# Merging one PSUM tile, moving one values step, and cutting the last output piece in three

## The chip, the cores and the metric

The kernel runs on one core of a Trainium2 chip. The metric is the device time in microseconds; before the change it is 170.12 us, the median of 3 runs (170.12 to 170.14). The engines named below are TensorE (PE, with its weight loads PEld), VectorE (DVE), ScalarE (ACT), GpSimd (POOL) and SyncE (SP). SP and ACT issue the output transfers, POOL the loads of the inputs.

## The reference, cut to what matters

Block-sorted attention over 4 batches with 8 heads of 768 positions, followed by a maxout layer. All inputs and the output are float32.

```python
P = sort_net                                   # (4, 8, 8, 8)
for _ in range(5):                             # Sinkhorn: rows, then columns
    P = np.exp(P - P.max(-1, keepdims=True))
    P = P / (P.sum(-1, keepdims=True) + 1e-09)
    P = P / (P.sum(-2, keepdims=True) + 1e-09)
k_sorted = np.einsum('bhij,bhjcd->bhicd', P, k_b)   # blocks of 96 positions
v_sorted = np.einsum('bhij,bhjcd->bhicd', P, v_b)
scores = scale * q_b @ k_sorted.T                   # within a block
attn = softmax(scores)
x = (attn @ v_sorted)                               # to (3072 tokens, 512)
h1, h2 = x @ w1, x @ w2                             # 512 -> 1024
out = np.maximum(h1, h2) @ w_out                    # 1024 -> 512
```

## The kernel before, in words

The maxout is computed as relu(x (W1 - W2)) Wout + x (W2 Wout). So the kernel needs, besides the difference of the two weights, the small product W2 Wout, 512 x 512, once. For it W2 is transposed on PE (`w2_transposes`, L525, in two calls of 16 transposes each, into the PSUM tiles `tw_ps` and from there into the SBUF tile `w2T`), and four products (`w_product`, L556, PSUM tile `wc_ps`) of eight matmuls of 512 columns each run over the eight row blocks of `w2T` in order and give the four parts of `wc`. The first call of `w2_transposes` fills row blocks 0 to 3 of `w2T`; the second, the one that the change touches, fills blocks 4 to 7.

All PSUM tiles come from one pool of four buffers, of two banks each, taken in turn (`psum`, L61). A tile can be taken only when what was read out of the tile four places before is through. A copy out of PSUM is `evac` (L98): on ACT at L103 or on DVE at L105.

A batch goes through sorting of K and V (`sort_k`, `sort_v`), scores and their exp (`scores`, eight units of a batch), attention times V (`values`, L463: eight matmuls, and on DVE a reciprocal and a multiplication that gives a part of `x`), the transposes of x (`x_transposes`, L496; of the first batch on PE through PSUM tile `tx_ps`, four calls), the hidden layer (`moe_h`, tiles `h_ps` and `g`) and the output (`moe_out`, tile `out_ps`, 12 matmuls for each 128 tokens: eight over `g` with Wout and four over the transposed x with `wc`). V is brought into another order before its sorting by copies on DVE, the turns (`turn_v`, L203; twelve positions of a block at a time for later batches, L707).

The order of the work is written by hand: each engine's instructions stand in the order in which the Python program issues them, and nothing moves them. In the loop over batches (L748) the units of a batch's maxout are issued one by one; after unit n come the steps of `tail[n]` (L716), and then as many steps of the next batch's attention as are due. In the first batch unit 3 is the last hidden unit of the first half of the tokens, units 4 and 5 are the first two W2 Wout products, and `tail[3]` holds, between them: values of unit 6, the second call of the W2 transposes, values of unit 7, a transpose of x, and three turns. The call has the letters "AD": the first eight transposes go to a PSUM tile of their own that ACT empties, the last eight to another that DVE empties.

The last 256 tokens of the last batch are put out in pieces by `moe_out_last` (L632): for each piece 12 matmuls over its columns into a PSUM tile, a copy on ACT (L640) or DVE (L642), and a DMA of the piece to the output (L643), issued from ACT where ACT copied and from SP otherwise. Before the change tokens 4 x 128 onward go as one piece of 512 columns, and the last 128 tokens as a piece of 384 columns on DVE and one of 128 columns on ACT.

Of the kernel before, what the change touches and what calls it, by code (L numbers as in the profile page):

```python
# [9 lines left out]

FP32 = mybir.dt.float32
BF16 = mybir.dt.bfloat16


@with_exitstack
def kernel(
# [16 lines left out]
    nc = tc.nc  # L33
# [4 lines left out]
    B, H, S, D = q.shape  # L38
# [26 lines left out]
    def ps_f32(name):  # L65
        return psum.tile([128, 1024], FP32, tag="ps", name=name)

    def ps_bf16(name):
        return psum.tile([128, 2048], BF16, tag="ps", name=name)

    fill = const.tile([128, 512], BF16, tag="fill", name="fill")
    nc.vector.memset(fill, 0.0)  # L72
# [11 lines left out]
    def late_zeros(by):  # L84
        late[by] = const.tile([128, 128], BF16, tag=f"late{by}", name="late")
        nc.vector.memset(late[by], 0.0)
# [11 lines left out]
    def evac(out_ap, in_ap, n, two_x=False, eng=None):  # L98
        a_ns, d_ns = (200 + n) / 1.2, (130 + (n / 2 if two_x else n)) / 0.96
        if eng:  # L100
            load[eng] += a_ns if eng == "A" else d_ns
        if (eng or pick(a_ns, d_ns)) == "A":
            nc.scalar.copy(out=out_ap, in_=in_ap)  # L103
        else:
            nc.vector.tensor_copy(out=out_ap, in_=in_ap)  # L105
# [9 lines left out]
    for b in range(2):  # L115
        kT[b] = big.tile([128, 32 * BLK + 32], BF16, tag=f"kT{b}", name="kT")
        kT[b + 2] = kT[b]
        nc.vector.memset(kT[b][:, 32 * BLK :], 0.0)
    v_dc = big.tile([128, D * BLK + 32], BF16, tag="v_dc", name="v_dc")
    nc.vector.memset(v_dc[:, D * BLK :], 0.0)  # L120
    e_bufs = []
    for n in range(NE):
        t = big.tile([BLK, 8 * BLK + 32], BF16, tag=f"e{n}", name=f"e{n}")
        nc.vector.memset(t[:, 8 * BLK :], 0.0)
# [34 lines left out]
    w2_sb = big.tile([128, HP, DFF], BF16, tag="w2", name="w2_sb")  # L159
# [16 lines left out]
    ident = const.tile([128, 128], BF16, tag="ident", name="ident")  # L176
# [26 lines left out]
    def turn_v(rows, eng, c0, c1, d0=0, d1=D):  # L203
        dst = v_dc[rows, 0 : D * BLK].rearrange("p (d c) -> p d c", c=BLK)[:, d0:d1, c0:c1]
        src = v_raw[rows].rearrange("p (c d) -> p d c", d=D)[:, d0:d1, c0:c1]
        if eng == "A":
            nc.scalar.copy(out=dst, in_=src)
        else:
            nc.vector.tensor_copy(out=dst, in_=src)  # L209


    rowsum = const.tile([G, NB], FP32, tag="rowsum", name="rowsum")
# [309 lines left out]
    w2T = big.tile([128, NFB, DMODEL], BF16, tag="w2T", name="w2T")  # L522
    wc = big.tile([128, HP, DMODEL], BF16, tag="wc", name="wc")

    def w2_transposes(t, eng):  # L525

        w = 16 // len(eng)
        outs = []
        for p, e in enumerate(eng):
            ps = ps_bf16("tw_ps")  # L530
            for n in range(w):
                fb, dmt = t * 4 + (p * w + n) // 4, n % 4
                nc.tensor.matmul(  # L533
                    ps[:, n * 128 : (n + 1) * 128],
                    w2_sb[:, dmt, fb * 128 : (fb + 1) * 128],
                    ident,
                    is_transpose=True,
                    start=True,
                    stop=True,
                )  # L540
            outs.append((ps, p, e))

        def out():
            for ps, p, e in outs:
                fb = t * 4 + p * w // 4
                evac(
                    w2T[:, fb : fb + w // 4, :].rearrange("p f d -> p (f d)"),
                    ps[:, 0 : w * 128],
                    w * 128,
                    two_x=True,  # L550
                    eng=e,
                )

        return out
# [77 lines left out]
    def moe_out_last(ti, pieces):  # L632

        tok0 = (B - 1) * S + ti * 128
        for n0, n1, eng in pieces:
            ps = ps_f32("out_ps")
            out_products(ps[:, 0 : n1 - n0], B - 1, ti, n0, n1)
            o = opool.tile([128, n1 - n0], FP32, tag=f"o{ti}{n0}", name="o", bufs=1)
            if eng == "A":
                nc.scalar.copy(out=o, in_=ps[:, 0 : n1 - n0])  # L640
            else:
                nc.vector.tensor_copy(out=o, in_=ps[:, 0 : n1 - n0])  # L642
            (nc.scalar if eng == "A" else nc.sync).dma_start(  # L643
                out=out[tok0 : tok0 + 128, n0:n1], in_=o
            )


    def att(b):

        SC = [lambda u=u: scores(b, u) for u in range(8)]  # L650
        VA = [lambda u=u: values(b, u) for u in range(8)]
        TR = [lambda t=t: x_transposes(b, t) for t in range(4)]
        return SC, VA, TR
# [20 lines left out]
    SC, VA, TR = att(0)  # L674
# [37 lines left out]
    def load_rest():  # L712
# [5 lines left out]
        2: [SC[6], SC[7], VA[5]],  # L718
        3: [
            VA[6],  # L720
            lambda: w2_transposes(1, "AD")(),
            VA[7],
            lambda: x_transposes(0, 2, "A"),
            lambda: [turn(second, c) for c in (0, 12, 24)],
        ],
# [22 lines left out]
    for b in range(B):  # L748
        units = [lambda t=t: moe_h(b, 0, t, None if b else "A") for t in range(4)]
        if b == 0:  # L750
            units[0] = lambda: None
            units[1] = lambda: None
        wps = [lambda dmt=dmt: w_product(dmt, "A" if dmt == 1 else None) for dmt in range(4)]
        if b == 0:
            units += wps[:2]
        units += [lambda t=t: moe_h(b, 1, t) for t in range(4)]
        cost = [1.3] * 8
        if b == 0:
            units += wps[2:]
            cost[4:4] = [1.7] * 2  # L760
            cost += [1.7] * 2
        units += [
            lambda ti=ti, part=part: moe_out(b, ti, part)
            for ti in range(6 if b < B - 1 else 4)
            for part in range(2)
        ]
        cost += [1.3] * 12
        if b == B - 1:
            units += [
                lambda: moe_out_last(4, [(0, 512, "D")]),  # L770
                lambda: moe_out_last(5, [(0, 384, "D"), (384, 512, "A")]),
            ]
        steps, lo = [], 2
        load["A"] = load["D"] = 0.0
        if b < B - 1:
            qs = [lambda half=half: q_transposes(1, half) for half in range(2)]
            if b < 2:
                tail[18 - 4 * b] = [lambda two=two: pair_q(b + 2, two) for two in range(2)]
                tail[18 - 4 * b] += [lambda half=half: q_transposes(b + 2, half) for half in range(2)]
            ks = [lambda t=t, b=b: sort_k(b + 1, t) for t in range(3)]  # L780
            SC, VA, TR = att(b + 1)

            def group(*fs):
                return [lambda: [f() for f in fs]]

            if b == 0:
                lo = 10
                tail[9][2:2] = ks
                vs = [lambda t=t: sort_v(1, t) for t in range(4)]
                tns = [lambda c=c: turn(both, c) for c in range(0, BLK, 12)]  # L790
                for step, n in [((VA, 0), 0), ((VA, 1), 1), ((VA, 2), 2), ((VA, 4), 3), ((TR, 1), 4), ((VA, 5), 5), ((SC, 7), 6), ((VA, 6), 7)]:
                    step[0][step[1]] = lambda f=step[0][step[1]], g=tns[n]: (f(), g())
                steps = group(*vs[:3]) + qs[:1] + group(*SC[0:2], vs[3]) + qs[1:] + VA[:1]
                steps += group(*SC[2:5]) + VA[1:2]
            elif b == 1:
                vs = [lambda t=t: sort_v_pair(2, t) for t in range(8)]
                steps = group(*ks) + group(*vs[:2]) + group(*SC[0:2], late_loads)
                steps += group(*vs[2:4]) + group(*vs[4:6]) + group(*vs[6:]) + group(*SC[2:4]) + VA[:2]
            else:
                steps = group(*ks) + group(*SC[0:2])  # L800
                steps += VA[:1] + group(*SC[2:5]) + VA[1:2]
            rest = SC[4:] if b == 1 else SC[5:]
            steps[-1:] = group(VA[1], TR[0])
            steps += VA[2:3] + group(VA[3], TR[1])
            steps += group(*rest[:-1]) + VA[4:5] + rest[-1:] + group(VA[5], TR[2])
            steps += VA[6:7] + group(VA[7], TR[3])
        done = 0
        for n, unit in enumerate(units):
            unit()
            for step in tail.get(n, []):  # L810
                step()
            total = sum(cost[lo:-2])
            want = -(-len(steps) * sum(cost[lo : n + 1]) // total)
            while done < min(want, len(steps)):
                steps[done]()
                done += 1
        tail = {}
# [28 lines left out]
```

The softmax here doesn't subtract the row's maximum and nothing guards it: scores larger than these inputs give would overflow.

## Time and profile before

| what | value |
|---|---|
| median of 3 runs | 170.12 us |
| profiled execution | 170.12 us, of it 168.3 us span (first to last instruction) |
| DVE, ACT busy | 92.2 us (55%), 80.2 us (48%) |
| chain that ended last, by engine | PE 90%, DVE 6%, DMA 1%, ACT 1%, issue 1% |
| chain, largest lines | out_ps L607 38%, h_ps L580 26%, wc_ps L559 4%, tw_ps L533 1% |
| granted PE clock | 1.00 |
| output DMAs at the end: 512, 384, 128 columns | 256, 192, 64 KB; 2.0, 1.9, 1.7 us from issue to landing |

The chain of waits is followed back from the last instruction, at each step to what released it. A timeline row gives start, length, engine, line, operation, written and read tiles, and in brackets the idle time before and what ended it. PE matmuls are pipelined, and their ends are modelled, so a group's length includes the run-out of its last matmul where another engine waits for it. A row with x8 merges eight instructions.

### The profile page before, as it was taken

What the parts mean: (1) busy time and instruction counts of PE and PEld (TensorE: products, weight loads), DVE (VectorE), ACT (ScalarE), POOL (GpSimd) and SP (SyncE); (2) the same over time, 40 slices, a digit from 0 to 9 for tenths busy, and PEclk for the clock granted to TensorE, in tenths of its full rate; (3) what the DMA queues carried; (4) which work ended last, traced back from release to release, by engine and by line L of the source; (5) the groups of instructions that cost most, each with busy time, mean ns of one, the idle gap of its engine ahead of it and who ended that gap; (6) DMA issues with size and microseconds to landing.
All of it is one profiled execution on the core that took longest, in us unless ns stands there. A gap on an engine that the chain in (4) does not pass through costs nothing.

```text
span 168.3 us, 4525 instructions
## 1 busy us (share of the span) xinstructions
PE 162.1 (96%) x2003; PEld 96.7 (57%) x2003; DVE 92.2 (55%) x198; ACT 80.2 (48%) x99; POOL 25.0 (15%) x40
## 2 busy tenths in 40 slices
PE   7799999999999999999999999999999999999992
PEld 7738766746666554457665545576554545654452
DVE  4979686699256589847674448074452322240041
ACT  3598976855874554046773350446605404311000
POOL 7954372124200000000500000000000000000000
PEclk9999999999999999999999999999999999999999
DMA  3999999999999864990199349930024183000333
GB/s 49 199 204 208 198 207 206 209 193 205 216 217 200 138 177 70 210 265 36 14 198 168 95 124 210 210 114 6 0 51 129 46 214 126 2 0 0 125 125 125
DMA packets 29666, 23.09 MB, mean 137 GB/s; under 512 B 16656, under 2 KB 24592, under 8 KB 29648
## 3 DMA queue, kind: packets, MB, share of 16 engines
q0 software_dynamic: 10304, 12.58, 44.2%
q1 hardware_dynamic: 19200, 10.17, 24.2%
q8 instruction: 15, 0.25, 0.6%
q10 hardware_dynamic: 144, 0.07, 0.1%
q14 instruction: 3, 0.02, 0.0%
HBM read 25.17 MB, written 6.29 MB: 187 GB/s over the span
## 4 chain that ended last, share of the span: by engine, by line
PE 90%; DVE 6%; DMA 1%; ACT 1%; issue 1%
PE out_ps L607 38%; PE h_ps L580 26%; PE o_ps L471 5%; PE wc_ps L559 4%; PE k_ps L377 4%; PE s_ps L444 4%; PE v_ps L398 2%; PE v_ps L419 1%; PE tw_ps L533 1%; DMA p_sb<-in_sort_net_dram 1%; PE tx_ps L509 1%; PE tq_ps L352 1%; PE tq_ps L347 1%; DVE colsum L226 1%; PE o_ps L81 1%
## 5 line engine op out<-in xcount | busy, mean ns | idle before, releaser
L607 PE MATMUL out_ps<-wo_sb,g 128*128 128x512 bf16 (+2 forms) x200 | 48.1, 371 | 0.0
L580 PE MATMUL h_ps<-xT,w_sb 128*128 128x384 bf16 x256 | 44.8, 326 | 0.2 <-ACT g L594 0.2
L580 PEld LDWEIGHTS <-w_sb 128*128 128x128 bf16 x256 | 24.0, 98 | 15.8 <-issue 0.2
L452 ACT ACTIVATE e<-s_ps 96x768 bf16<-96x768 f32 x32 | 24.2, 804 | 16.1 <-PE s_ps L444 15.9
L607 PEld LDWEIGHTS <-g 128*128 128x128 bf16 x200 | 17.0, 97 | 15.7
L594 ACT ACTIVATE g<-h_ps 128x768 bf16<-128x768 f32 x21 | 16.9, 811 | 18.4 <-PE h_ps L580 18.4
L607 PE MATMUL out_ps<-wc,xT 128*128 128x512 bf16 (+2 forms) x100 | 24.8, 370 | 0.0
L103 ACT COPY o<-out_ps 128x1024 f32<-128x1024 f32 x9 | 9.1, 1012 | 30.0 <-PE out_ps L607 25.7
L596 DVE TENSOR_SCALAR g<-h_ps 128x768 bf16<-128x768 f32 x11 | 10.5, 955 | 22.6 <-PE h_ps L580 22.6
L488 DVE TENSOR_TENSOR x<-o_ps,rs 96x512 bf16<-96x512 f32 x32 | 22.0, 686 | 1.1
L482 DVE RECIPROCAL rs<-o_ps 96x8 f32<-96x8 f32 x32 | 6.4, 200 | 19.8 <-PE o_ps L471 19.8
L607 PEld LDWEIGHTS <-xT 128*128 128x128 bf16 x100 | 9.6, 97 | 11.2
L209 DVE COPY v_dc<-v_raw 64x768 bf16<-64x768 bf16 (+2 forms) x18 | 15.6, 898 | 0.4 <-DMA v_raw<-in_v_dram 0.3
L471 PEld LDWEIGHTS <-e 96*128 96x128 bf16 x256 | 11.7, 97 | 6.6 <-ACT e L452 0.5
L471 PE MATMUL o_ps<-v_sb,e 96*128 96x65 bf16 x256 | 13.1, 193 | 0.1
L105 DVE CAST v_sb<-v_ps 96x1024 bf16<-96x1024 f32 x7 | 8.5, 1213 | 4.7 <-PE v_ps L398 4.2
L103 ACT CAST v_sb<-v_ps 96x1024 bf16<-96x1024 f32 x9 | 8.9, 1013 | 1.1 <-PE v_ps L419 1.0
L444 PEld LDWEIGHTS <-kT 64*128 64x128 bf16 x256 | 6.0, 94 | 5.3 <-issue 4.6
L444 PE MATMUL s_ps<-qT,kT 64*128 64x96 bf16 x256 | 8.5, 204 | 0.1
L81 PEld LDWEIGHTS <-fill 128*128 128x128 bf16 x109 | 7.1, 122 | 2.2 <-DVE fill L72 1.2
L105 DVE COPY o<-out_ps 128x1024 f32<-128x1024 f32 x2 | 2.5, 1225 | 10.6 <-PE out_ps L607 9.5
L103 ACT CAST kT<-k_ps 128x1024 bf16<-128x1024 f32 x8 | 7.7, 1021 | 1.1 <-PE k_ps L377 1.1
(76 smaller groups left out, 138.3 us busy)
## 6 DMA issues: line engine op xcount, KB each, us to landing
out_dram<-o SPq DMA_DIRECT2D x11, 512.0 KB, 3.1
k_raw<-in_k_dram POOLq DMA_DIRECT2D x12, 256.0 KB, 10.4
q_raw<-in_q_dram POOLq DMA_DIRECT2D x4, 768.0 KB, 12.5
v_raw<-in_v_dram POOLq DMA_DIRECT2D x6, 384.0 KB, 13.6
w_sb<-in_moe_w_dram POOLq DMA_DIRECT2D x3, 512.0 KB, 15.8
wo_sb<-in_moe_w_out_dram POOLq DMA_DIRECT2D x2, 512.0 KB, 19.5
v_raw<-in_v_dram POOLq DMA_DIRECT2D x3, 256.0 KB, 4.9
w_sb<-in_moe_w_dram POOLq DMA_DIRECT2D x2, 256.0 KB, 14.1
```

Source lines behind the costliest of these rows:

```text
L81: nc.tensor.matmul(ps[:, 0:w], w0, fill[:, 0:w], start=True, stop=True)
L103: nc.scalar.copy(out=out_ap, in_=in_ap)
L105: nc.vector.tensor_copy(out=out_ap, in_=in_ap)
L209: nc.vector.tensor_copy(out=dst, in_=src)
L444: nc.tensor.matmul(ps[:, h2 * 512 + ii * 128 : h2 * 512 + ii * 128 + BLK], kT[b][rows, (hp * 8 + i) * BLK : (hp * 8 + i) * BLK + 128], rhs ...
L452: nc.scalar.activation(out=e[:, 0 : 8 * BLK].rearrange("p (t c r) -> p t c r", t=8, r=R), in_=ps[0:BLK].rearrange("p (t f) -> p t f", t=8) ...
L471: nc.tensor.matmul(ps[:, h2 * 512 + ii * 65 : h2 * 512 + (ii + 1) * 65], e[:, (h2 * 4 + ii) * BLK : (h2 * 4 + ii) * BLK + 128], v_sb[:, m0 ...
L488: nc.vector.tensor_tensor(out=x, in0=ov[:, :, :, 0:D], in1=rs.to_broadcast([BLK, 2, 4, D]), op=ALU.mult,)
L580: nc.tensor.matmul(h_ps[t][:, m * 512 : m * 512 + TCH], w1_sb[:, hp, fb * 128 : (fb + 1) * 128], xT[:, b % 2, ch, hp % 2, hp // 2, :], sta ...
L594: nc.scalar.activation(out=g, in_=src, func=AF.Relu)
L596: nc.vector.tensor_scalar(out=g, in0=src, scalar1=0.0, scalar2=None, op0=ALU.max)
L607: nc.tensor.matmul(dst, g_tiles[b, ch, m // 2][:, m % 2, off : off + 128] if m < NFB else xT[:, b % 2, ch, hp % 2, hp // 2, off : off + 12 ...
```

## The change

Four edits. `turn_v` gets a repeat loop with a count of 1. `w2_transposes` takes one PSUM tile for all sixteen transposes of a call, and copies it out in as many column ranges as the call has letters; for the first call (one letter) that is what it did before, for the second ("AD") two tiles of eight transposes become one tile with two copies. In `tail[3]` the values of unit 7 are issued ahead of that second call, no longer behind it. The last 128 tokens go out in three pieces of 256, 128 and 128 columns, on ACT, DVE and ACT, in place of two of 384 and 128 on DVE and ACT.

```diff
+TWICE = 1
...
-        if eng == "A":
-            nc.scalar.copy(out=dst, in_=src)
-        else:
-            nc.vector.tensor_copy(out=dst, in_=src)
+        for _ in range(TWICE):
+            if eng == "A":
+                nc.scalar.copy(out=dst, in_=src)
+            else:
+                nc.vector.tensor_copy(out=dst, in_=src)
...
     def w2_transposes(t, eng):
-
-        w = 16 // len(eng)
-        outs = []
-        for p, e in enumerate(eng):
-            ps = ps_bf16("tw_ps")
-            for n in range(w):
-                fb, dmt = t * 4 + (p * w + n) // 4, n % 4
-                nc.tensor.matmul(
...
-            outs.append((ps, p, e))
-
+        ps = ps_bf16("tw_ps")
+        for n in range(16):
+            fb, dmt = t * 4 + n // 4, n % 4
+            nc.tensor.matmul(
...
         def out():
-            for ps, p, e in outs:
-                fb = t * 4 + p * w // 4
+            w = 2048 // len(eng)
+            for n, e in enumerate(eng):
                 evac(
-                    w2T[:, fb : fb + w // 4, :].rearrange("p f d -> p (f d)"),
-                    ps[:, 0 : w * 128],
-                    w * 128,
+                    w2T[:, t * 4 : t * 4 + 4, :].rearrange("p f d -> p (f d)")[
+                        :, n * w : (n + 1) * w
+                    ],
+                    ps[:, n * w : (n + 1) * w],
+                    w,
                     two_x=True,
                     eng=e,
                 )
...
             VA[6],
+            VA[7],
             lambda: w2_transposes(1, "AD")(),
-            VA[7],
             lambda: x_transposes(0, 2, "A"),
...
-                lambda: moe_out_last(5, [(0, 384, "D"), (384, 512, "A")]),
+                lambda: moe_out_last(5, [(0, 256, "A"), (256, 384, "D"), (384, 512, "A")]),
```

More of the change, by code (lines that the diff above doesn't have):

```diff
@@ L525, in w2_transposes @@
     def w2_transposes(t, eng):
-        w = 16 // len(eng)
-        outs = []
-        for p, e in enumerate(eng):
-            ps = ps_bf16("tw_ps")
-            for n in range(w):
-                fb, dmt = t * 4 + (p * w + n) // 4, n % 4
[L533 to L540, printed above, removed]
-            outs.append((ps, p, e))
+        ps = ps_bf16("tw_ps")
+        for n in range(16):
+            fb, dmt = t * 4 + n // 4, n % 4
+            nc.tensor.matmul(
+                ps[:, n * 128 : (n + 1) * 128],
+                w2_sb[:, dmt, fb * 128 : (fb + 1) * 128],
+                ident,
+                is_transpose=True,
+                start=True,
+                stop=True,
+            )
         def out():
-            for ps, p, e in outs:
-                fb = t * 4 + p * w // 4
+            w = 2048 // len(eng)
+            for n, e in enumerate(eng):
                 evac(
-                    w2T[:, fb : fb + w // 4, :].rearrange("p f d -> p (f d)"),
-                    ps[:, 0 : w * 128],
-                    w * 128,
+                    w2T[:, t * 4 : t * 4 + 4, :].rearrange("p f d -> p (f d)")[
[3 more added lines that the diff above has]
+                    w,
                     two_x=True,
```

## The prediction

> **What bounds the kernel now.** I read the page's first two parts, then the chain of waits, then the timeline at the two places that the change touches, last the DMA view of the end.
>
> ```profile
> span 168.3 us, 4525 instructions
> PE 162.1 (96%) x2003; PEld 96.7 (57%) x2003; DVE 92.2 (55%) x198; ACT 80.2 (48%) x99; POOL 25.0 (15%) x40
> ```
>
> TensorE (PE) is busy 96% of the span, and the row PEclk of the page is full in every slice. From 38 to 113 us the chain is PE alone; so whatever PE loses or gains at one place is carried to the end, unless a later PE wait absorbs it, and there are only two small ones (0.07 us at 113.89, about 0.2 us at 117.5 behind an activation that itself follows PE). The rest of the span is the start (12.6 us), and what follows the last product. First place, the chain in the stretch of 30 to 40 us (start, length, what):
>
> ```profile
> 32.46 0.90 PE tw_ps L533 x16
> 33.36 0.24 PE o_ps L471 x8
> 33.60 0.39 PE tx_ps L509 x8
> 34.00 0.02 issue
> 34.02 1.89 PE wc_ps L559 x8
> 35.91 0.34 PE tx_ps L509 x8
> 36.25 1.73 PE wc_ps L559 x8
> ```
>
> The reader is to see two unequal twins: the first W2 Wout product with its gap takes 1.91 us and the second 1.73, the tx group before it 0.39 against 0.34. PE loses 0.19 + 0.05 = 0.24 us here. The timeline of 29 to 40 us tells why:
>
> ```profile
> 32.96 1.01 ACT L103 COPY w2T<-tw_ps 128x1024 bf16<-128x1024 bf16 x1
> 33.40 0.69 DVE L105 COPY w2T<-tw_ps 128x1024 bf16<-128x1024 bf16 x1
> 34.23 0.69 DVE L488 TENSOR_TENSOR x<-o_ps,rs 96x512 bf16<-96x512 f32 x1
> 35.25 3.03 DVE L209 COPY v_dc<-v_raw 64x768 bf16<-64x768 bf16 x4 [0.33 <-DMA v_raw<-in_v_dram]
> ```
>
> The two copies overlap. The first wc_ps is the fourth PSUM tile after the one that the ACT copy reads; with four buffers it takes the same one, and starts at 34.02, just after that copy's end (33.97). Second place, the end, in the timeline from 161 us:
>
> ```profile
> 163.76 0.81 PE L607 MATMUL out_ps<-wc,xT 128*128 128x384 bf16 x4
> 164.41 0.61 PE L607 MATMUL out_ps<-wo_sb,g 128*128 128x128 bf16 x8
> 164.61 0.56 DVE L642 COPY o<-out_ps 128x384 f32<-128x384 f32 x1 [1.26 <-PE out_ps L607]
> 165.28 0.27 ACT L640 COPY o<-out_ps 128x128 f32<-128x128 f32 x1 [9.33 <-PE out_ps L607]
> 165.57 0.37 ACTq L643 DMA_DIRECT2D out_dram<-o  x1
> ```
>
> The last 128 columns go PE, ACT, DMA. In the DMA windows of 166.5 to 166.6 (two lines) and 166.8 to 166.9 (one), with packets, MB and share of the 16 DMA engines, q1 is SP's queue with the 384-wide piece, and q10 is ACT's:
>
> ```profile
> q1 hardware_dynamic: 26, 0.03, 84.0%
> q10 hardware_dynamic: 8, 0.00, 13.6%
> ...
> q10 hardware_dynamic: 39, 0.01, 51.0%
> ```
>
> The last small piece starts while the wide one still fills the engines. The last bytes move at 166.92, and the span ends 1.38 us later with no data moving.
>
> **What the Trainium skill says.** "PSUM — Partial Sum Buffer", sections "Specifications (TRN2)" and "PSUM bank collisions raise a hardware error": a bank holds 2 KiB per partition, two engines must not be on the same bank at once, and different banks are free. The halves of the merged tile (1024 bf16 each) are two banks, so the chip would let both copies run together; before, the copies overlap from 33.40 to 33.97 out of two tiles. No trace of before shows two copies out of one tile. "DMA: Bandwidth & Descriptors", section "Anatomy of one DMA — SWDGE (gpsimd) path": a fixed part of about 2 us, mostly the confirmation of the last write. That section is for POOL's path; here the three last output pieces, from SP and ACT, land 1.7 to 2.0 us after issue, with sizes of 64 to 256 KB, so the fixed part rules here too. Its section "Issuing engines are not separate DMA queues" says that they all share 16 engines and interleave: the shares of q1 and q10 above show it.
>
> **The change, part by part.**
>
> 1. The repeat count of 1 in turn_v adds nothing. No W2 Wout product changes its tile, and no turn moves; what changes are the second half of the W2 transposes, the place of one values step, and the last output piece.
>
> 2. The middle. PE has the same instructions, values(7) now ahead of the transposes. In the built program's order both copies now hang on each other: ACT's waits for the sixteenth transpose (before: the eighth), VectorE's (DVE) for ACT's copy (before: for its own eight transposes). One PSUM tile fewer is taken, so the first wc_ps now takes the buffer of values(6), free at 33.43: the bank wait goes. Step by step, on the clock of the trace of before:
> values(6) ends at 32.46. Its successor values(7) needs the exp that ended at 32.11, and runs to 32.70 (0.24). The transposes run to 33.60 (0.90), tx to 33.94 (0.34). The x multiplication of values(7) follows its twin on DVE from 33.43 and is through about 34.35, no cover lost.
> ACT starts at 33.64 (hop 0.04, as from wc_ps at 35.91 to its copy at 35.95) and ends at 34.65 (1.01). DVE follows at 34.68 and ends at 35.37 (0.69).
> The first wc_ps matmul could start at 33.78 (a group's last matmul has its modelled end 0.16 after the next may start). At 0.216 each, the fifth would start at 34.64; it needs ACT's half, at 34.69: +0.05. The seventh would then start at 35.12; it needs DVE's half, at 35.42: +0.30. The eighth starts at 35.64 and ends at 36.02. Before: 35.91. So +0.11 us: 0.24 of old waits go, 0.35 of new ones come.
> What stands behind: ACT's tx copy moves from 34.03 to about 34.66 and ends at 35.46, ahead of the wc copy at about 36.06, and its first reader is at 38.1. The DVE turns start at 35.37 in place of 35.25, their v_raw having landed; four of them end 0.12 later at 38.4, and the block-diagonal work behind them has its reader (sort_k) at 43.4. DVE idles 2.27 us before 44.40, waiting for a load of q, which absorbs it. POOL's load of v_raw at 42.42 waits for a turn and moves by 0.1. No PE wait for such a load is in the chain.
> The unknown is the size of the hand-overs and whether the new waits cost what their copies last. Lower bound -0.24 (all old waits go, none comes: it needs DVE's half by 35.1). Upper bound +0.45: three hops of 0.15 in place of 0.04. I take +0.11.
>
> 3. The end. Twelve 384-wide products become twelve of 256 and twelve of 128. Spacings in the trace: 384 wide, (164.41 - 162.46) / 12 = 162.5 ns; 128 wide, 0.45 / 8 = 56; six of 512 take 1.30, so 216. For 256 the skill's formula ("TensorE: Matmul & The Clock Gate", section "Back-to-back issue gap", N / 2.4 + 2.5) gives 109, and it fits the other three. 12 x (109 + 56 - 162.5) = +0.03 us. The twelve more weight loads hide: 98 ns each in the row of L607, yet the 128-wide products go every 56.
> ACT's 256-wide copy is not in this trace; 266 ns for 128 and 0.59 us for 512 (wc at 35.95) give an estimate of 0.37. It runs 163.97 to 164.34, its DMA issue to 164.73, and ACT then waits for the last copy until 165.31: 0.58 us of cover. The DVE piece of 128, 0.29 by the slope between its 512 and 384 copies (691 and 558 ns), ends at 164.93. The third tile takes a buffer that DVE emptied at 161.36. No wait.
> Bytes follow an issue by 0.85 us (163.38 to 164.23, and 165.20 to 166.05 in the DMA windows). So the 128 KB move from about 165.2 to 165.6, the middle 64 KB from 165.8 to 166.1, and the last 64 KB, issued at 165.60, from 166.45, alone: 0.23 us of each engine (15.3% of 1.5 us in the DMA view of 165.8 to 167.3) and 0.11 of stagger (the 256 KB took 0.80 for 0.69 busy) end at 166.79. Before: 166.92. So the piece that finishes last gains 0.13 net of the 0.03. Bounds: gain 0.24 (no stagger, net) and loss 0.03 (its start was never delayed by the wide piece).
>
> Sum: +0.11 - 0.13 = -0.02 us. The profiled execution took 170.12 us itself (span 168.3 and 1.8 around it), the median of the runs: 170.1 us.
>
> **Rivals.** I call no change what lies within 0.2%, 0.34 us, about what this measurement tells apart.
> A, slower: the new chain transposes, ACT, DVE, PE is longer than the sum of its rows. For it: three hand-overs in series where PE had the two copies side by side, and no row for two copies of one tile. Against it: hops of 0.02 to 0.05 everywhere in the chain. With 0.15 a hop the middle costs 0.45, and with no gain at the end 170.12 + 0.45 + 0.03 = 170.6 us. It decides once DVE's half is ready 0.2 us later than 35.42.
> B, faster: PE finds both halves in time, as it would if ACT did start after eight transposes, and the last piece gains its whole 0.24: 170.12 - 0.24 - 0.24 = 169.64 us. For it: the bank wait really goes. Against it: the wait for the sixteenth transpose.
> C, the end loses its gain alone because the piece's own latency set it: +0.11 + 0.03, 170.26 us, still no change.
>
> **How the numbers follow.** Forecast with C on its edge: 0.66 in all, 169.85 to 170.4. A: 0.23, since a chain in series has more ways to grow than to shrink. B: 0.11. The range reaches to A's 170.55 and, on the other side, to 169.75. Faster 0.11, same 0.66, slower 0.23.
>
> **What would show it.** In the changed trace: DVE's w2T copy starts after ACT's has ended, about 34.7, with ACT named as its releaser; the first wc_ps group lasts about 2.1 us, its start near 33.95; ACT's 256-wide copy near 164.0; q1 and q10 no longer share a window at the end; last bytes about 1.2 us after the last ACT issue and not 1.35. Wrong it would be if PE shows a wait over 0.5 us before the first wc_ps ends, or if the last piece lands 1.7 us after issue as now.

## The result, and the profile after

The changed kernel takes 170.85 us, the median of 6 runs (170.41 to 171.02), against 170.13 us for the kernel before beside it: a ratio of 1.0042, with a 95% interval of 1.0029 to 1.0055. It is slower by 0.72 us. The profiled execution took 171.01 us, of it 169.2 us span, 0.9 us more than the span before.

That 0.9 us has two places. The first is the middle; this is the chain of waits of the changed kernel from 30 to 40 us:

```profile
32.23 0.49 PE o_ps L473 x16
32.71 0.91 PE tw_ps L531 x16
33.62 0.02 issue
33.65 1.02 ACT w2T L104
34.67 0.02 issue
34.69 0.70 DVE w2T L106
35.39 0.05 issue
35.44 0.60 PE wc_ps L557 x2
36.05 0.34 PE tx_ps L511 x8
36.39 1.73 PE wc_ps L557 x8
```

The chain, which ran on PE alone here before, now leaves PE for the two copies of `w2T`, one behind the other, and comes back for the last two of the eight products (x2). The tx group that follows starts at 36.05 in place of 35.91, so PE is 0.14 us late, and it stays so: the second W2 Wout product, and every later group of the chain up to the last pieces, has the same shift. The twelve more products at the end add 0.03.

The other 0.72 us come after PE has stopped. The timeline of the changed kernel, last rows:

```profile
165.45 0.27 ACT L638 COPY o<-out_ps 128x128 f32<-128x128 f32 x1 [0.97 <-PE out_ps L605]
165.75 0.61 ACTq L641 DMA_DIRECT2D out_dram<-o  x1
```

The last copy starts 0.17 us later than before (0.14 + 0.03), and so does its issue, give or take 0.01. From that issue to the end of the span it was 168.3 - 165.57 = 2.73 us before; now it is 169.2 - 165.75 = 3.45. The DMA view from 155 us on (KB each, and us from issue to landing) shows why:

```profile
out_dram<-o SPq DMA_DIRECT2D x1, 256.0 KB, 4.0
out_dram<-o ACTq DMA_DIRECT2D x1, 128.0 KB, 3.4
out_dram<-o SPq DMA_DIRECT2D x1, 64.0 KB, 3.0
out_dram<-o ACTq DMA_DIRECT2D x1, 64.0 KB, 2.5
```

All four last pieces land late, the 256 KB one too, which the change doesn't touch (2.0 us before). And queue q8, which the profile calls the instruction queue, moves one packet here that was not there before: a piece of the program itself. The page of the kernel before and that of the changed one have these lines for q8, over the whole run:

```profile
q8 instruction: 15, 0.25, 0.6%
```

```profile
q8 instruction: 16, 0.26, 0.6%
```

The sixteenth packet, of some 16 KB (0.25 MB / 15), is the new one; the windows of the changed kernel put it between 164 and 165 us, where it takes 8.2% of 16 engines for 1 us, 1.3 us of a single engine:

```profile
q1 hardware_dynamic: 111, 0.23, 59.1%
q8 instruction: 1, 0.02, 8.2%
```

From 166.3 to 166.8 us only four output packets start, at 5.7% of the engines' time, a little less than one engine of sixteen (6.25%), as a single engine that is behind would give them:

```profile
q1 hardware_dynamic: 4, 0.01, 5.7%
```

The packet list of the same trace says whose they are. The 256 KB piece goes in 128 packets of 2 KB. 120 of them are over by 165.19; the last eight start one behind another from 165.96 to 166.91, and the fetch ran from 164.66 to 165.97. Eight of 128 is the share of one engine of sixteen. The last output packet ends at 167.7 us; before, nothing moves after 167. PE itself does not wait for the fetch: ACT's last copy, which follows PE's last product, starts at 165.45, while the fetch is still under way.

The Trainium skill, "Runtime: NRT & Kernel Launch", section "Instruction fetch mechanics", says that an engine's instructions are brought in by DMA in blocks of 16 KiB, 256 instructions each, and that crossing into a new block is "mostly hidden". The size agrees with q8. Whether the crossing is hidden here is what the experiments are about.

### The profile page after: what moved, and what is told of

Read it like the earlier page. It is cut to its first block, busy times and chain, and to the rows that moved or that the text cites. A ratio compares the mean times of both kernels' runs of the same rounds, so it can differ in the third digit from the quotient of the medians.

```text
span 169.2 us, 4552 instructions
## 1 busy us (share of the span) xinstructions
PE 161.7 (96%) x2015; PEld 96.7 (57%) x2015; DVE 91.9 (54%) x198; ACT 80.6 (48%) x100; POOL 25.6 (15%) x40
## 4 chain that ended last, share of the span: by engine, by line
PE 88%; DVE 6%; ACT 2%; DMA 1%; issue 1%
PE out_ps L605 37%; PE h_ps L578 26%; PE o_ps L473 5%; PE k_ps L379 4%; PE s_ps L446 4%; PE wc_ps L557 3%; PE v_ps L400 2%; PE v_ps L421 1%; PE tw_ps L531 1%; DMA p_sb<-in_sort_net_dram 1%; PE tq_ps L354 1%; PE tq_ps L349 1%; DVE colsum L228 1%; PE o_ps L82 1%; PE tx_ps L511 1%
## 5 line engine op out<-in xcount | busy, mean ns | idle before, releaser
L605 PEld LDWEIGHTS <-g 128*128 128x128 bf16 x208 | 17.6, 97 | 15.2
L557 PE MATMUL wc_ps<-wo_sb,w2T 128*128 128x512 bf16 x32 | 7.8, 380 | 0.1
```

The source lines that it names most:

```text
L557: nc.tensor.matmul(ps[:, 0:512], w2T[:, fb, dmt * 128 : (dmt + 1) * 128], wo_sb[:, fb, :], start=(fb == 0), stop=(fb == NFB - 1),)
L605: nc.tensor.matmul(dst, g_tiles[b, ch, m // 2][:, m % 2, off : off + 128] if m < NFB else xT[:, b % 2, ch, hp % 2, hp // 2, off : off + 12 ...
```

## The experiments

Theory F: the program has 4008 instructions for PE before and 4032 after (the profiles show 4006 and 4030 of them). The 24 more are 12 products with their weight loads; with them PE's program calls for one more block, the fetch of this block falls among the last output pieces, and one DMA engine hands in its share of them late. Rivals: M, the middle costs more than its trace shows; Q, three pieces with two issues on ACT's queue cost by themselves. In each table row the time of the kernel before is that of the same chip. The last two columns are of the profiled run: the packets of q8, and the time from the last output issue to the end, good to 0.05 us, as spans are given to a tenth.

| run | us | before | ratio, 95% interval | fetches | last issue to end of span, us |
|---|---|---|---|---|---|
| m1_middle_only | 170.16 | 169.97 | 1.0001 to 1.0017 | 15 | 2.70 |
| t1_tail_only | 170.66 | 169.97 | 1.0021 to 1.0044 | 16 | 3.27 |
| a1_after_fewer | 170.03 | 169.97 | 1.0000 to 1.0016 | 15 | 2.52 |
| b1_before_more | 170.64 | 169.97 | 1.0025 to 1.0049 | 16 | 2.67 |
| b2_split_matmuls | 170.68 | 170.00 | 1.0024 to 1.0054 | 16 | 3.71 |
| a2_after_more_late | 170.07 | 170.00 | 0.9995 to 1.0016 | 16 | 2.52 |
| c1_one_copy | 169.78 | 170.00 | 0.9980 to 0.9993 | 15 | 2.65 |
| c2_one_copy_three | 169.70 | 170.00 | 0.9981 to 1.0005 | 15 | 2.54 |
| c3_one_copy_three_late | 169.71 | 170.02 | 0.9977 to 0.9990 | 16 | 2.52 |

**The two halves of the change apart.** m1 is the changed kernel with the two pieces of before:

```diff
-                lambda: moe_out_last(5, [(0, 256, "A"), (256, 384, "D"), (384, 512, "A")]),
+                lambda: moe_out_last(5, [(0, 384, "D"), (384, 512, "A")]),
```

> The changed kernel with the last 128 tokens in the two pieces of before, so that only the merged PSUM tile and the moved values step are left; PE has 4008 instructions as before. Theory F (the extra time of the changed kernel comes from one more 16 KB instruction fetch, which falls into the output transfers at the end): no such fetch at the end, last piece landing in about 1.7 us, only the middle's own loss of 0.14 us: 170.2 to 170.3. Rival M (the middle costs more than its trace shows): 170.7 or above.

0.19 us slower by the medians (interval 0.02 to 0.29), and the end takes what it took before (2.70 us). So the middle costs what its chain shows, 0.14, as nearly as this can tell, and M falls. t1 is the opposite, the kernel before with the three pieces:

> The kernel before with the last 128 tokens in three pieces; PE has 4032 instructions as the changed one. Theory F: the fetch of 16 KB stands between 163 and 165.5 us, the last pieces land 2.5 us or more after issue, time 170.5 to 170.9. Rival M: no change or a small gain, 170.0 to 170.2. Rival Q (three pieces with two issues on ACT's queue cost in themselves): 170.5 to 170.9 as well; the next run tells F from Q.

0.69 us slower, without any change in the middle. The fetch starts between 164.0 and 164.25 us, and the last piece lands after 2.4 us. Both F and Q say so.

**The same three pieces without the block.** a1 is the changed kernel with fewer warm-up matmuls at its start:

```diff
-keep_streaming(ps_f32("fill_ps"), 18 * 512, width=96)
+keep_streaming(ps_f32("fill_ps"), 18 * 512, width=110)
```

> The changed kernel with its first warm-up matmuls 110 in place of 96 columns wide, 84 in place of 96 of them: 24 PE instructions fewer, 4008 as before, three pieces kept. Theory F: no fetch after 150 us, last piece landing in 1.5 to 1.7 us, time 170.0 to 170.25, 0.6 to 0.9 below the changed kernel. Rivals M and Q: 170.7 to 171.0 as the changed kernel.

170.03 us: with 24 instructions fewer at the start of the kernel, the three pieces at its end no longer cost. The last one lands in 1.6 us, and from its issue to the end are 2.52 us, some 0.2 less than before. Q falls, F stands. Of its 22 runs four lie between 170.45 and 170.92; see b1.

**More instructions at the start of the kernel before.** b1 has 86 in place of 96 in the same line, which makes 108 matmuls of 96:

> The kernel before with its first warm-up matmuls 86 in place of 96 columns wide, 108 in place of 96: 24 PE instructions more, 4032 as the changed kernel, nothing else different. Theory F: a fetch of 16 KB between 163 and 165.5 us, the last pieces landing 2.3 us or more after issue, time 170.5 to 171.0. Rivals M and Q: 170.1 as before.

The time came as F has it, but not by F's way, so this run does not count for it. The sixteenth fetch starts between 162.75 and 163.0 us, earlier than F's forecast: the 24 instructions stand ahead of the work of the end here, so PE comes to any given number of its instructions at an earlier point of that work. The 256 KB piece lands in 2.9 us, yet the last two take 1.9 and 1.7 as before. The time was lost elsewhere: in this timeline (PE alone) PE stands for half a microsecond early on, with nothing that it waits for in the profile:

```profile
19.88 0.22 PE L444 MATMUL s_ps<-qT,kT 64*128 64x96 bf16 x2 [0.50 <-issue]
```

It is taken up again under "What the runs showed".

**The products alone.** b2 leaves pieces, copies and DMAs of the kernel before as they are, and only does the 384-wide products in two parts:

```diff
-out_products(ps[:, 0 : n1 - n0], B - 1, ti, n0, n1)
+for c0, c1 in [(0, 256), (256, 384)] if n1 - n0 == 384 else [(n0, n1)]:
+    out_products(ps[:, c0 - n0 : c1 - n0], B - 1, ti, c0, c1)
```

> The kernel before, with the twelve 384-wide products of the last 128 tokens done as twelve of 256 and twelve of 128 into the same PSUM tile; the DVE copy of 384 columns, its DMA and everything else stay. So the PE instructions are those of the changed kernel's end (4032), the pieces and queues those of before. Theory F (instruction fetch at the end): a 16 KB fetch between 163 and 165 us, the last two pieces landing 2.3 us or more after issue, time 170.5 to 170.9. Rival Q (three pieces, two issues on ACT's queue): no change, 170.0 to 170.2.

170.68 us (the profiled run, 171.14, is the longest of the six). PE, DVE and ACT are at the end within 0.02 us of before (last issue at 165.59), but the landings are not. Two lines of the DMA view from 164 to 166 us, then three from 155 on:

```profile
q1 hardware_dynamic: 135, 0.25, 32.3%
q8 instruction: 1, 0.02, 5.8%
```

```profile
out_dram<-o SPq DMA_DIRECT2D x1, 256.0 KB, 4.3
out_dram<-o SPq DMA_DIRECT2D x1, 192.0 KB, 3.0
out_dram<-o ACTq DMA_DIRECT2D x1, 64.0 KB, 2.8
```

The same pieces on the same queues took 2.0, 1.9 and 1.7 us before; now they take 1.6 to 2.2 times as long. Again the last eight of the 128 packets of the 256 KB piece start only when the fetch ends (166.2 us). Here nothing differs but twelve products more, 0.02 us of PE's time, and their 24 instructions; it costs 0.68 us.

**More instructions still, so that the fetch comes earlier.** a2 is the changed kernel, with the products of two earlier tiles of 128 tokens in halves:

```diff
-out_products(ps[:, slot * 512 : (slot + 1) * 512], b, ti, part=part)
+if b == B - 1 and ti in (2, 3):
+    n0 = part * 256
+    out_products(ps[:, slot * 512 + n0 : slot * 512 + n0 + 256], b, ti, n0, n0 + 256)
+else:
+    out_products(ps[:, slot * 512 : (slot + 1) * 512], b, ti, part=part)
```

> The changed kernel with 48 PE instructions more: the products of tokens 2 x 128 to 4 x 128 of the last batch in halves of 256 columns, which costs 24 x 2.5 ns = 0.06 us. Three pieces kept. Theory F: the sixteenth fetch comes some 5 us earlier, before 161 us, and is over before the last pieces; the last one lands in 1.5 to 1.7 us; 170.1 to 170.4, below the changed kernel in spite of more instructions. Rival Q: 170.8 to 171.0. A rival that every further PE instruction costs by itself: above 171.0.

170.07 us: with 48 instructions more than the changed kernel, only 0.07 us above the kernel before, where the changed one was 0.72 above it. One run of its 13 is at 170.92. The one q8 packet of its end lies in the window of 160 to 161.5 us (first line), with nothing beside it, and takes 3.9% of 16 engines for 1.5 us, 0.94 us of one. The pieces land as they should (from 155 us on):

```profile
q8 instruction: 1, 0.02, 3.9%
```

```profile
out_dram<-o SPq DMA_DIRECT2D x1, 256.0 KB, 2.0
out_dram<-o ACTq DMA_DIRECT2D x1, 128.0 KB, 1.8
out_dram<-o SPq DMA_DIRECT2D x1, 64.0 KB, 1.6
out_dram<-o ACTq DMA_DIRECT2D x1, 64.0 KB, 1.6
```

So it is not the fetch itself that costs, but where it falls: a2 has sixteen too. This is shown. No record names the DMA engine that carries a packet; that the fetch and the late packets share one is inferred, from the eight packets of 128 that start when the fetch ends.

**The middle, mended.** c1 is the kernel before with the one PSUM tile of the change (its `w2_transposes`), but with one DVE copy of all 2048 columns, ahead of the values step. The call differs from that of the kernel before in this:

```diff
-            lambda: w2_transposes(1, "AD")(),
+            lambda: w2_transposes(1, "D")(),
             VA[7],
```

A line behind it, left out here, keeps the sums by which the program shares the copies out to ACT and DVE as they were, so that no other copy changes its engine.

> The kernel before with the second call of the W2 transposes in one PSUM tile as in the change, but with one copy of 2048 columns on DVE for its two, ahead of the values step as before; two pieces at the end. The bank wait of the first W2 Wout product goes, and no copy waits for another: DVE's copy should run 33.4 to 34.7, the fifth product then waits under 0.1 us. Theory of the middle (waits as in the trace): 0.15 to 0.2 us below the kernel before, 169.75 to 169.9. If the middle's waits are covered later: as before, 170.0.

169.78 us, below the kernel before by 0.22 (interval 0.12 to 0.34). In its timeline and in its chain of 30 to 40 us:

```profile
33.46 1.22 DVE L105 COPY w2T<-tw_ps 128x2048 bf16<-128x2048 bf16 x1
```

```profile
33.67 0.34 PE tx_ps L509 x8
34.01 1.77 PE wc_ps L555 x8
35.78 0.34 PE tx_ps L509 x8
36.12 1.73 PE wc_ps L555 x8
```

The twins (the two W2 Wout products with the tx groups ahead of them) are now equal to 0.04 us. From the first tx group to the second it is 2.11 us (33.67 to 35.78) in place of 2.31 (33.60 to 35.91), so 0.20 us of waits are gone, though this profiled run (169.97) is the longest of c1's 21. One copy of 1.22 us is ready sooner than two of 1.01 and 0.69 in series.

**Both gains together.** c2 adds to c1 the three pieces and the 84 warm-up matmuls of a1.

> The one-copy kernel with the three pieces at the end and 84 warm-up matmuls in place of 96, so that PE has 4008 instructions. Theory F together with the gain of the end (0.2 us from the last issue to the end of the span, as the run with fewer instructions showed) and of the middle: 169.6 to 169.75, below both kernels. If the three pieces gain nothing: 169.8 to 169.9.

The median is 169.70, but with runs up to 170.62, and the interval takes in no change. Its profiled run (170.40 us) is one of the long ones, and its timeline of PE has the pause of b1:

```profile
21.37 0.28 PE L444 MATMUL s_ps<-qT,kT 64*128 64x96 bf16 x5 [0.49 <-issue]
```

c3 therefore leaves the warm-up alone, and takes the fetch off the last pieces as a2 does.

> The one-copy kernel with the three pieces at the end and, as in the run with 48 instructions more, the products of tokens 2 x 128 to 4 x 128 of the last batch in halves of 256 columns; the warm-up stays at 96 matmuls. Theory F: sixteenth fetch near 160 us, off the last pieces; PE pays 0.09 us for 36 more products; no pause of PE at its 701st instruction, which the run with 84 warm-up matmuls showed; 0.2 us gained at the end: 169.6 to 169.75, and no runs near 170.4. If the early pause is not a matter of where the instruction blocks end, runs near 170.4 come here too.

169.71 us, from 169.55 to 170.00 in 21 runs, none near 170.4: faster than the kernel before by 0.31 us (interval 0.9977 to 0.9990), where the changed one was slower by 0.72. Its sixteenth fetch starts between 159.75 and 160 us, and the last piece lands in 1.6 us.

## Why the prediction was wrong, point by point

Forecast were 170.1 us and no change, in a range of 169.75 to 170.55; it came to 170.85, 0.72 us slower than before.

The middle (step 2) held. ACT's copy was put at 33.64 to 34.65, and DVE's at 34.68 to 35.37; they ran from 33.65 and from 34.69, with DVE's wait named after ACT. The seventh product was put at 35.42 and came at 35.44. The loss was put at 0.11 and is 0.14; m1 shows it alone (0.19 by the medians). The hand-overs are 0.02 to 0.05 us, so the series of rival A had no more to give than its rows. A's 170.6 us is nearer to the result than the forecast, but by a mechanism that did not happen. (The old wait is 0.23 us by the rows shown, and not 0.24: 1.91 - 1.73 is 0.18.) Whether two copies could run side by side out of one PSUM tile, as the prediction held, no run shows.

Of the end (step 3) the sizes held: 0.03 us for the twelve more products, 0.37 us for ACT's copy of 256 columns, 0.29 for DVE's of 128, no wait for a PSUM tile. For 256 columns the prediction took N / 2.4 + 2.5. The Trainium skill, "TensorE: Matmul & The Clock Gate", section "Back-to-back issue gap", gives this formula for a single matmul, and 81 ns at 128 columns and 131 at 512 for streams of weight loads and matmuls. In the streams of this kernel the spacing was 56 ns at 128, 109 at 256 (162.60 to 163.47 us for eight) and 216 at 512: the formula fits, the figures for streams do not.

The gain of the last piece was put at 0.16 us behind its issue. Without the fetch it is 0.17 to 0.19 by the unrounded spans of the traces (a1, a2, c3), and it came about as forecast: in a1 the last bytes have moved 1.20 us after the last ACT issue, with q1 through before they start. c3 was 0.31 us below the kernel before where c1 was 0.22, though PE does 36 products more in c3 (an estimated 36 x 2.5 ns = 0.09 us). This points the same way, but the intervals of the two overlap.

The step that failed is the sentence on the twelve added products with their weight loads, that they cost 12 x (109 + 56 - 162.5) ns, and that the loads hide. That is all they cost on PE. But they are also 24 instructions, and with them comes a sixteenth fetch, over the same 16 DMA engines that carry the output. b2 has just these products and costs 0.68 us; the sum put this at nothing, without a term for it, and no rival named it. The page of before showed that there are such fetches: q8, with 15 of them, which the prediction does not mention. The landing of the last piece, which the prediction named as the sign of being wrong if it stayed at 1.7 us, rose to 2.5.

So the 0.72 us of the medians is the middle's 0.14, the products' 0.03 and the fetch, less the pieces' gain of some 0.18; that leaves about 0.7 us for the fetch, as b2 has it. In the profiled run, one of the longer ones, the end alone lost 0.72, which is the gain of 0.18 given up and some 0.9 us of fetch.

## What to carry to other kernels

An edit that adds instructions to a long unrolled program can bring one more instruction fetch, and if that falls where the last outputs leave, its cost has nothing to do with the edit's own work: count the engine's instructions, compare the fetches on the instruction queue, and look at when the last one comes. A test of such an edit should add or take away instructions elsewhere, as a1 and a2 do, or add them alone, as b2 does, before the edit itself is blamed. And two copies that run side by side out of two PSUM tiles become two in series when they share one, as they did here, where DVE's copy waited for ACT's; one copy of the whole (1.22 us) then beat both.

## What the runs showed of the hardware that was not expected

A fetch takes 0.94 us of one DMA engine with nothing beside it (a2), 1.3 us among output packets in the changed kernel and 1.86 in b2. Behind it the landing of the four last output pieces was 2.5 to 4.0 us (the changed kernel) in place of 1.6 to 2.0 (a1). "Mostly hidden", as the skill says of crossing a block, holds for the sixteenth fetch of a2 and c3, but not for that of the changed kernel. What the other fifteen cost no run shows.

PE also stood still where the profile shows no wait. In b1 and c2, which have 24 warm-up instructions more and fewer, it does so for 0.5 us, in different work at different times (19.4 and 20.9 us), yet behind the same instruction in each: the weight load that is number 701 in the order of PE's matmuls and weight loads. That a block ends there is a guess that was not tried; with the 256 instructions to a block of the skill's "Instruction fetch mechanics" the same grid has a boundary at 701 + 13 x 256 = 4029 (an estimate), between the 4008 of the kernel before and the 4032 of the changed one, which fits. Why only some runs of a1 and c2 are long was not settled either: their medians don't show the pause, and c2's profiled run does. c3, with the warm-up of before, has no long run in 21, but a2, with the same warm-up, has one in 13.
